# Attention's list scheduler: what a task waits for when its forerunner runs on the same engine

## The chip, the core and the metric

The program runs on one core of a Trainium2 chip, as one launch. The metric is the device time of the whole program in microseconds (us). The core has a matrix engine (TensorE, PE in the profile, its weight loads PEld), three element-wise engines (VectorE, DVE; ScalarE, ACT; GpSimd, POOL) and queues that issue DMAs, here above all SyncE's (SP). Each engine works through its own list of instructions in order; semaphores tie the lists together.

## The reference

Three layers follow each other; the output of one is the input of the next.

```python
scores = scale * np.matmul(q, k.transpose(0, 1, 3, 2))      # B, H, S, D = 4, 8, 576, 64
scores = np.where(causal, -1e9, scores) - rowmax
a = np.exp(scores); a /= a.sum(-1, keepdims=True) + 1e-09
local = np.matmul(a, v)
mem_out = (phi(q) @ M_prev) / (phi(q) @ z_prev + 1e-06)
attn = g * mem_out + (1 - g) * local
# x: 2304 tokens of 512 values
# layer 2: tokens with x @ w_skip > 0 go to the best of 8 experts (512 -> 1024 -> 512), weighted, added to x
# layer 3: leaky_relu(x @ w_in) @ w_out, 512 -> 2048 -> 512
```

## The kernel before

**Attention.** The 32 pairs of batch and head are worked on as 8 groups of 4 heads. For each group K and Q are loaded, split into a coarse part and a remainder (L592, L599), transposed on PE (L644, L647) and copied out of PSUM by ACT (L665, L666, L672). Each head then has two slots, one for the first two blocks of 128 rows and one for the other three. A slot runs this chain: PE makes scores (`mm`, L728); DVE adds the mask and takes row maxima (`mx`, L735) and writes them beside Q (`sp`, L747 and L752); PE transposes that (`q2t`, L759) and ACT copies it out (`q2e`, L764); PE makes the scores a second time, transposed and with the maximum taken off (L779, L781, the diagonal's mask L786 and L790); ACT takes the exponential (`exp`, L795); PE multiplies by V (`pv`, L817 and L820), with outputs 64 columns of the array wide, where nearly all other matmuls use 128. Two heads share a `pv` result. When it is complete, three DVE tasks follow each other: `f1` (L857, L859), `f2` (L864) and `f4` (L872, L874); POOL adds the two halves (L882).

Beside this, ACT, DVE and POOL turn the third layer's weights into another format (`conv_chunk`, L321 to L341); finished rows are routed to experts (`route_blk`, L925 to L946, with outputs 32 and 64 columns wide in L934 and L943; `route`, L972 to L1035). Towards the end the first expert's weights are split (L438, L444) and its first two tiles are computed (`early`, L485 to L531), with rows fetched by a gather (L1106, then transposed by L1119) that needs the table which the routing scatters write (L1035).

**What sets the order.** All of this is put down as 2159 tasks, each with an engine, an assumed duration, the tasks it depends on, a due time (`key`), and buffers that it takes and gives back. `Sched.order` plays them through: whenever an engine is free it starts the ready task with the smallest key for which buffers are free. A finished task makes its dependents ready `LAT` later: 550 ns after PE, 180 after ACT, 170 after DVE, 240 after POOL, 2300 after SP, or a latency of the task's own. The instructions are then issued in the order of these starts. The result is only an order for each engine; on the chip each instruction waits for its real semaphores.

The tasks that have a forerunner on their own engine are: on PE the `pv` steps of a slot and the first expert's products; on ACT the second copy of a K tile after the first (L666 after L665) and the successive `exp` of a slot; on DVE the `mx` of a slot, then `sp`, and `f1`, `f2`, `f4`; on POOL the routing scatters.

**After attention** come the experts (L1119 to L1266, in blocks chosen by the count of each expert's tokens) and the third layer (L1511 to L1617); their order doesn't go through the scheduler.

Of the kernel before, what the change touches and what calls it, by code (L numbers as in the profile page):

```python
# [34 lines left out]
SP = [[[(0, 0, 0, 128), (1, 128, 0, 256)]], [[(2, 0, 0, 384)], [(3, 0, 0, 512)], [(4, 0, 0, 256)], [(4, 0, 256, 320)]]]  # L35
# [28 lines left out]
class Sched:  # L64
# [9 lines left out]
    def order(self):  # L74
        ts, free = self.tasks, dict(self.free)
        users = [[] for _ in ts]
        left = [len(t[3]) for t in ts]
        for i, t in enumerate(ts):
            for d in t[3]:
                users[d].append(i)  # L80
        ready = {e: [] for e in self.LAT}
        busy = {e: 0.0 for e in self.LAT}
        ev, out = [], []

        def wake(i):
            heapq.heappush(ready[ts[i][0]], (ts[i][4], i))
        for i in range(len(ts)):
            if not left[i]:
                wake(i)
        now = 0.0  # L90
        while len(out) < len(ts):
            moved = True
            while moved:
                moved = False
                for e, rd in ready.items():
                    if busy[e] > now or not rd:
                        continue
                    skip = []
                    while rd:
                        key, i = heapq.heappop(rd)  # L100
                        eng, dur, fn, deps, _, take, give, lat = ts[i]
                        if all(free[p] >= 1 + (p == "s" and key > now + AHEAD) for p in take):
                            for p in take:
                                free[p] -= 1
                            end = now + dur
                            busy[e] = end
                            heapq.heappush(ev, (end, -1, None))
                            heapq.heappush(ev, (end + (self.LAT[e] if lat is None else lat), i, give))
                            out.append((now, i))
                            moved = True  # L110
                            break
                        skip.append((key, i))
                    for x in skip:
                        heapq.heappush(rd, x)
            if not ev:
                raise RuntimeError("stuck")
            now = ev[0][0]
            while ev and ev[0][0] <= now:
                _, i, give = heapq.heappop(ev)
                if i < 0:  # L120
                    continue
                for p in give:
                    free[p] += 1
                for u in users[i]:
                    left[u] -= 1
                    if not left[u]:
                        wake(u)
        self.end = now
        return [i for _, i in out]

# [1570 lines left out]
```

## Time and profile before

| | us |
|---|---|
| time, median of 3 runs | 864.18 (863.03 to 865.46) |
| the profiled execution's own time | 864.59 |
| its span, first to last instruction | 863.0 |
| PE busy | 829.5 (96%) |
| DVE, ACT, POOL busy | 612.4, 482.4, 193.4 |

The profile comes from one execution. Busy time counts instructions at work; a matmul's end is modelled, so that a row's end may lie beyond the next row's start, and the distance from start to start is the safer reading. In rows of a timeline a line's equal neighbours are merged (x12 is twelve of them), and the time in brackets is how long the engine sat idle ahead of them. A float32 matmul of `pv` is two records in the trace and one in the program. Attention lasts from 0 to about 298 us, mixed with the first expert's tiles to 329 us; the experts follow to 466 us, the third layer from there to the end.

### The profile page before, as it was taken

The numbers are of one execution on the slowest core, as the hardware profiler recorded it, in microseconds if no ns is written. First come the engines' busy times: TensorE is split into PE (matmuls) and PEld (weight loads), VectorE is DVE, ScalarE is ACT, GpSimd is POOL, SyncE is SP. The second block draws the span as 40 slices with busy tenths as digits, with TensorE's granted clock in tenths as the row PEclk, the third lists the DMA queues.
The fourth block names the chain that finished last, engine by engine and source line by source line (L and its number), as shares of the span: only waits on it lengthen the run. The fifth ranks groups of instructions, "written<-read, shape, count | busy, mean of one in ns | idle before, by whom it ended". The sixth has DMA issues, their size and how long they took to land. (4 is left out here: it accounts for less than half of the span.)

```text
span 863.0 us, 19512 instructions
## 1 busy us (share of the span) xinstructions
PE 829.5 (96%) x7368; PEld 739.8 (86%) x7368; DVE 612.4 (71%) x1739; ACT 482.4 (56%) x937; POOL 193.4 (22%) x262
## 2 busy tenths in 40 slices
PE   6999999999999898999989999999999999999997
PEld 5788888887887776677568999999999999999997
DVE  6878888788869964775674699665656565656564
ACT  8898978887866643765564465333333333333332
POOL 6545536445524423130220000000000000000000
PEclk9999999999999999999999999999999999999999
DMA  6867665856375768795833201010101010101000
GB/s 145 218 158 224 163 201 139 220 191 130 124 251 182 267 232 269 269 353 207 282 144 134 74 1 51 1 51 1 51 1 49 2 49 2 50 2 49 1 26 25
DMA packets 103946, 107.61 MB, mean 125 GB/s; under 512 B 69661, under 2 KB 69789, under 8 KB 103828
## 3 DMA queue, kind: packets, MB, share of 16 engines
q1 hardware_dynamic: 101190, 100.90, 37.5%
q0 software_dynamic: 2640, 5.21, 1.8%
q8 instruction: 67, 1.10, 0.5%
q14 instruction: 49, 0.40, 0.1%
HBM read 81.57 MB, written 25.86 MB: 124 GB/s over the span
## 5 line engine op out<-in xcount | busy, mean ns | idle before, releaser
L1616 PE MATMUL g<-sw,ah 128*128 128x256 f32 x448 | 126.0, 281 | 0.0
L1615 PE MATMUL g<-sw,ah 128*128 128x256 f32 x448 | 125.7, 281 | 0.0
L1567 DVE SCALAR_TENSOR_TENSOR ua<-ua 128x512 f32<-128x512 f32 x72 | 49.7, 690 | 80.2 <-ACT ua L1516 80.2
L1516 ACT ACTIVATE ah<-ua 128x384 fp32r<-128x384 f32 (+1 forms) x72 | 38.8, 539 | 110.4 <-PE g L1617 71.2
L1516 ACT ACTIVATE ua<-t 128x512 f32<-128x512 f32 x72 | 43.0, 597 | 101.0 <-PE t L1560 101.0
L735 DVE CUSTOM_DVE_ANT_0 v<-t,v 128x512 f32<-128x512 f32 (+4 forms) x160 | 75.5, 472 | 28.4 <-PE t L728 22.8
L1617 PE MATMUL g<-sw,al 128*128 128x256 f32 x320 | 89.8, 281 | 0.0
L1615 PEld LDWEIGHTS g<-sw,ah 128*128 128x128 f32 x448 | 84.4, 188 | 0.0
L1616 PEld LDWEIGHTS g<-sw,ah 128*128 128x128 f32 x448 | 84.3, 188 | 0.0
L795 ACT ACTIVATE pT<-t 128x384 f32<-128x384 f32 (+2 forms) x128 | 62.5, 503 | 23.8 <-PE t L786 12.8
L1557 PE MATMUL t<-x,v 128*128 128x256 f32 x288 | 71.9, 283 | 0.7 <-ACT x L1436 0.7
L1558 PE MATMUL t<-x,a 128*128 128x256 f32 x288 | 71.0, 280 | 0.5 <-DVE a L1103 0.5
L1558 PE MATMUL t<-x,v 128*128 128x256 f32 x288 | 71.1, 279 | 0.0
L1557 PE MATMUL t<-x,a 128*128 128x256 f32 x288 | 71.0, 280 | 0.0
L820 PE MATMUL pv<-vn,pT 128*64 128x65 f32 x1280 | 61.7, 231 | 0.6 <-issue 0.6
L1617 PEld LDWEIGHTS g<-sw,al 128*128 128x128 f32 x320 | 60.9, 190 | 0.0
L820 PEld LDWEIGHTS pv<-vn,pT 128*64 128x64 f32 x1280 | 47.0, 138 | 16.1 <-issue 11.1
L338 POOL TENSOR_TENSOR cg<-cg,v 128x512 int32<-128x512 int32 x32 | 42.5, 1329 | 65.3 <-issue 38.8
L1557 PEld LDWEIGHTS t<-x,v 128*128 128x128 f32 x288 | 54.3, 188 | 1.2 <-ACT x L1436 0.9
L1558 PEld LDWEIGHTS t<-x,a 128*128 128x128 f32 x288 | 54.1, 188 | 0.7 <-DVE a L1103 0.7
L1558 PEld LDWEIGHTS t<-x,v 128*128 128x128 f32 x288 | 54.1, 188 | 0.3
L1557 PEld LDWEIGHTS t<-x,a 128*128 128x128 f32 x288 | 54.1, 188 | 0.0
(371 smaller groups left out, 2313.2 us busy)
## 6 DMA issues: line engine op xcount, KB each, us to landing
c<-in_moe_w_dram SPq DMA_DIRECT2D x32, 512.0 KB
va<-in_moe_w_dram SPq DMA_DIRECT2D x21, 512.0 KB
v<-in_moe_w_in_dram SPq DMA_DIRECT2D x16, 512.0 KB
v<-in_moe_w_out_dram SPq DMA_DIRECT2D x16, 512.0 KB
xe<-x SPq DMA_DIRECT2D x18, 256.0 KB
out_dram<-xe SPq DMA_DIRECT2D x18, 256.0 KB
a<-in_k_dram SPq DMA_DIRECT2D x32, 128.0 KB
a<-in_q_dram SPq DMA_DIRECT2D x32, 128.0 KB
```

What stands on the lines that cost most here:

```text
L338: nc.gpsimd.tensor_tensor(u["g"], u["g"], u["s"], op=ALU.add)
L735: nc.vector.tensor_tensor_reduce(out=self.y[:R, 0:w], in0=s[:R, o:o + w], in1=self.mb[:R, max(0, MB[i] + c0):max(0, MB[i] + c0) + w], scal ...
L795: nc.scalar.activation(u["pT"][:, o1:o1 + w], u.pop(("t", p))[:, 0:w], AF.Exp, scale=0.125)
L820: nc.tensor.matmul(t[m:m + 64, o:o + 65], u["pT"][:, c + m:c + m + 64], vn[:, j, h], start=(j == 0), stop=(j == i))
L1516: tt_, cp = V.tensor_tensor, lambda o, i: A.activation(o, i, AF.Copy)
L1557: nc.tensor.matmul(o, wih[k][:, fs], xh[:, k], start=(k == 0), stop=False)
L1558: nc.tensor.matmul(o, wil[k][:, fs], xh[:, k], start=False, stop=False)
L1567: V.scalar_tensor_tensor(u, u, 0.01, u, op0=ALU.mult, op1=ALU.max)
L1615: nc.tensor.matmul(o, ah, wh, start=(p == z == 0), stop=False, skip_group_check=True)
L1616: nc.tensor.matmul(o, ah, wl, start=False, stop=False, skip_group_check=True)
L1617: nc.tensor.matmul(o, al, wh, start=False, stop=(p == 7), skip_group_check=True)
```

## The change

When a task ends, an event is now put down for its own engine at the very end of the task, beside the one after the latency. Dependents on the same engine (all but SP) are released by the first event, all others by the second, which also gives the buffers back.

```diff
-                            heapq.heappush(ev, (end, -1, None))
+                            heapq.heappush(ev, (end, -1 - i, ()))
                             heapq.heappush(ev, (end + (self.LAT[e] if lat is None else lat), i, give))
...
                 _, i, give = heapq.heappop(ev)
-                if i < 0:
-                    continue
+
+                own, i = i < 0, max(i, -1 - i)
                 for p in give:
                     free[p] += 1
                 for u in users[i]:
-                    left[u] -= 1
-                    if not left[u]:
-                        wake(u)
+                    if (ts[u][0] == ts[i][0] != "SP") == own:
+                        left[u] -= 1
+                        if not left[u]:
+                            wake(u)
```

No instruction is added or left out; the order on each engine changes. From the diff on, lines of the changed kernel have numbers higher by one (L820 is L821 there).

On PE, here is the third batch's last group, between the transposes of K and Q (L644) and those of the finished rows (L925). In the rows, pv is the result of the product with V, t any other PSUM tile, 64x65 its 64 columns of the array and 65 columns of V. Before:

```order
L644 MATMUL t<-idr,v_84 128x128 x4
L728 MATMUL t<-b_86 128x384
L820 MATMUL pv<-vn_90,pT 64x65 x6
L728 MATMUL t<-b_86 128x512
L820 MATMUL pv<-vn_90,pT 64x65 x8
L759 MATMUL t<-idr,v_84 66x128 x3
L728 MATMUL t<-b_86 128x256
L728 MATMUL t<-b_86 128x320
L820 MATMUL pv<-vn_90,pT 64x65 x2
L728 MATMUL t<-c_88 128x384
L817 MATMUL pv<-vn_90,pT 64x65 x5
L779 MATMUL t<-b_86 128x192
```

and in the changed kernel:

```order
L645 MATMUL t<-idr,v_84 128x128 x4
L760 MATMUL t<-idr,v_84 66x128 x3
L729 MATMUL t<-b_86 128x384
L818 MATMUL pv<-vn_90,pT 64x65 x5
L729 MATMUL t<-b_86 128x512
L821 MATMUL pv<-vn_90,pT 64x65 x12
L729 MATMUL t<-b_86 128x256
L729 MATMUL t<-b_86 128x320
L780 MATMUL t<-b_86 128x192
L782 MATMUL t<-q_4402,b_86 128x192
```

Four stretches of pv with other work between them have become two, one of them of twelve matmuls; L759 has moved ahead of the scores.

On DVE, near the end of attention, stand f1 (its last line is L859), f2 (L864) and f4 (L872, L874) of a pair of heads, with the row maxima (L735, an operation and a read of its accumulator) of other slots. Before:

```order
L857 TENSOR_TENSOR pv<-pv,ev 64x130
L859 SCALAR_TENSOR_TENSOR nl_99<-t,gl 128x3x2
L859 SCALAR_TENSOR_TENSOR nl_99<-pv,gl 128x3x2
L735 ISA v_85,m_98<-t,v_85 128x128
L735 ISA m_98 128x1
L735 ISA v_85,m_98<-t,v_85 128x256
L735 ISA m_98 128x1
L864 RECIPROCAL rl<-nl_99 128x12
L735 ISA v_85,m_97<-t,v_85 128x128
```

and in the changed kernel:

```order
L858 TENSOR_TENSOR pv<-pv,ev 64x130
L860 SCALAR_TENSOR_TENSOR nl_99<-t,gl 128x3x2
L860 SCALAR_TENSOR_TENSOR nl_99<-pv,gl 128x3x2
L865 RECIPROCAL rl<-nl_99 128x12
L873 TENSOR_TENSOR xb<-pv,rl 128x3x128
L875 TENSOR_TENSOR m_4865<-t,rl 128x384
L736 ISA v_85,m_98<-t,v_85 128x128
```

The three tasks of a pair of heads now follow each other with nothing between, and the next slot's maxima stand behind them.

## Rows read from the trace of the kernel before

**Rows 1.** The page: busy us and share of PE; granted clock in 40 slices.
```profile
PE 829.5 (96%) x7368; PEld 739.8 (86%) x7368; DVE 612.4 (71%) x1739; ACT 482.4 (56%) x937; POOL 193.4 (22%) x262
...
PEclk9999999999999999999999999999999999999999
```

**Rows 2.** Windows: length, busy of PE, PEld, DVE, ACT, POOL, clock, DMA share.
```profile
20.00:100.00 80.00, 78.20 (x904) 65.80 (x904) 64.49 (x246) 73.54 (x168) 43.47 (x54) 1.00 0.71 190
100.00:200.00 100.00, 97.19 (x1219) 82.72 (x1219) 84.29 (x331) 84.09 (x189) 51.93 (x64) 1.00 0.68 187
200.00:290.00 90.00, 86.97 (x1095) 74.19 (x1095) 73.62 (x282) 65.25 (x144) 43.43 (x48) 1.00 0.54 167
290.00:330.00 40.00, 35.74 (x263) 27.50 (x261) 28.84 (x89) 16.16 (x28) 11.65 (x16) 0.96 0.71 251
330.00:466.00 136.00, 126.86 (x584) 91.03 (x584) 89.02 (x104) 81.77 (x117) 29.70 (x21) 0.99 0.70 247
466.00:863.00 397.00, 391.60 (x3232) 387.03 (x3232) 258.75 (x651) 144.21 (x257) 0.97 (x1) 1.00 0.09 31
```

**Rows 3.** Waits of PE from 20 to 298 us: total us, times, longest.
```profile
PE t L1119 <- DMA xe<-xs,ixe: 2.2, 1, 2.2
...
PE t L759 <- DVE v L752: 0.6, 2, 0.3
```

**Rows 4.** Timeline of PE, 242 to 253 us: start, length, instruction.
```profile
242.65 0.29 PE L786 MATMUL t<-negi,tri 128*128 128x256 bf16 x1
242.70 0.74 PE L728 MATMUL t<-b 128*128 128x512 f32 x3
...
247.52 0.69 PE L820 MATMUL pv<-vn,pT 128*64 128x65 f32 x16
248.14 0.38 PE L759 MATMUL t<-idr,v 128*66 128x128 f32 x3
...
250.44 0.30 PE L781 MATMUL t<-q,b 66*128 66x320 f32 x1
250.58 0.28 PE L786 MATMUL t<-negi,tri 128*128 128x256 bf16 x1
250.80 0.57 PE L820 MATMUL pv<-vn,pT 128*64 128x65 f32 x12
251.30 0.41 PE L779 MATMUL t<-b 128*128 128x320 f32 x1
...
252.12 0.31 PE L781 MATMUL t<-q,b 66*128 66x320 f32 x1
252.36 0.45 PE L820 MATMUL pv<-vn,pT 128*64 128x65 f32 x8
252.75 0.38 PE L759 MATMUL t<-idr,v 128*66 128x128 f32 x3
```

**Rows 5.** Timeline of DVE, 274 to 288 us.
```profile
274.09 0.17 DVE L859 SCALAR_TENSOR_TENSOR nl<-pv,gl 128x6 f32<-128x6 f32 x1
274.17 0.28 DVE L735 CUSTOM_DVE_ANT_0 v<-t,v 128x128 f32<-128x128 f32 x1
274.38 0.08 DVE L735 DVE_READ_ACCUMULATOR2_ANT m<- 128x1 f32 x1
274.50 0.42 DVE L735 CUSTOM_DVE_ANT_0 v<-t,v 128x256 f32<-128x256 f32 x1
...
286.85 0.16 DVE L859 SCALAR_TENSOR_TENSOR nl<-pv,gl 128x6 f32<-128x6 f32 x1
287.04 0.23 DVE L864 RECIPROCAL rl<-nl 128x12 f32<-128x12 f32 x1
```

**Rows 6.** Waits of DVE from 20 to 290 us.
```profile
DVE v L735 <- PE t L728: 24.0, 31, 2.5
```

**Rows 7.** Timelines of POOL and DVE near the end of attention.
```profile
280.00 1.72 POOL L1035 DMA_INDIRECT tbl<-r_tok,r_sli  x1 [0.16 <-issue]
...
289.62 3.42 DVE L444 TENSOR_TENSOR v<-a,v 128x1024 fp32r<-128x1024 f32 x1 [0.24 <-ACT v L438]
```

## The prediction

> **What bounds the kernel now.** I read the page first, then windows, then the waits of PE, then its timeline from start to start. The page shows PE busy for 96% of the span and at the full clock nearly throughout [rows 1]; it is the engine to watch. The windows show that this holds in every stage: from 20 to 290 us, which is attention, PE is busy for 78.20 + 97.19 + 86.97 = 262.4 of 270 us, among the experts for 126.86 of 136 us, in the third layer for 391.60 of 397 us [rows 2]. So two things decide the change: how much PE work attention holds, and the 7.6 us in which PE is idle there. The last two stages are not reordered, and as PE fills them, what attention saves or loses should reach the end about one for one.
>
> Of the 7.6 us of idle time the longest piece is one wait of 2.2 us for a gather near the end; waits that name DVE's `sp` as the releaser are two, 0.6 us in all [rows 3]. A kernel with so few waits can't win much by losing them. What the order can still change is PE's own work, and that shows only in the timeline read from start to start. Three stretches of `pv` matmuls, of 16, 12 and 8, last 0.62, 0.50 and 0.39 us until the next kind of matmul starts [rows 4]. From 8 to 16 that is (0.62 - 0.39) / 8 = 0.029 us each; so 0.39 - 8 x 0.029 = 0.16 us comes once per stretch (0.15 by the stretch of 12). Going in costs too: L786 is followed by an L728 after 0.05 us but by `pv` after 0.22 us, and L781 by L786 after 0.14 us but by `pv` after 0.24 us [rows 4]. That is 0.10 to 0.17 us more. So each separate stretch of `pv` costs 0.25 to 0.33 us of PE beside its matmuls. The idle columns of the waits don't show it, since the modelled ends of the matmuls cover it.
>
> **The change part by part.** *Fewer stretches.* A `pv` step depends on the one before it. Before, 550 ns of assumed latency kept it back and the scheduler filled in other work; now it can follow at once. In the two orders of PE, up to the first branch, I count 128 stretches of `pv` before and 95 after, about 3 fewer in each 75 tasks all through attention. The routing's narrow stretches (L934, L943) rise from 27 to 33, some of them next to `pv`; stretches of 128-wide work between narrow ones fall from 144 to 113. So 31 go-and-return pairs go. I take 0.25 us, the lower value, because entries from other lines are not in these rows: 31 x 0.25 = -7.7 us, with ends at 31 x 0.21 = -6.5 (if an entry hides a further 0.04) and 31 x 0.33 = -10.2.
>
> The Trainium skill bears on the count, in "TensorEngine Tiling (Array Packing)", section "Tiling Modes", under "Key Properties": a change of the tiling mode, and not only of the tile, drains the engine. The 0.15 us at each stretch's end agrees. By the rule a change between 64 and 32 columns, or between 64 and 128 rows, counts as well; all changes of mode in the orders fall from 305 to 250, which is 27.5 pairs and would make the term -6.9 us.
>
> *DVE.* `f1`, `f2`, `f4` stand together in 64 of 64 places, before in 21. When the follower needs the result, it starts 0.19 us after its forerunner (286.85 to 287.04); an independent one starts after 0.08 us (274.09 to 274.17) [rows 5]. So 43 more dependent starts x 0.11 = 4.7 us of DVE. DVE is busy for 222.4 of these 270 us [rows 2] and stands 24.0 us waiting for PE's scores [rows 6]; that hides it, and I cost it at nothing. Without that cover it would be up to +4.7 us. In the same way L666 now stands right behind L665 and `exp` behind `exp` on ACT; the same operations in another order, no cost by itself.
>
> *ACT as the next limit.* From 20 to 100 us ACT is busy for 73.54 of 80 us [rows 2]. PE's saving there would be 7.7 x 80 / 270 = 2.3 us; with 6.5 us of ACT idle time it fits, but in-order queues at over 90% seldom close all gaps. I give back 1.0 us (ends 0 and 2.3).
>
> *Less room ahead of q2t.* The row maxima of a slot are a chain on DVE. After the accumulator read at 274.38 the next maximum starts at 274.50, 0.12 us later [rows 5]. The old latency of 170 ns stood in for that; now the scheduler counts nothing, and puts `q2t` (L759) earlier on PE than DVE can serve it. What is queued behind a waiting L759 is all of PE. Ends: -1 us (the other loops gain room, since `q2e` to the second scores lies further apart now) and 64 q2t x 0.2 = +12.8 us. I take +2.0 us, a quarter more than today's 7.6 us idle, since DVE has time to run ahead.
>
> *The gather at the end.* The last routing scatter of batch 2 is issued at 280.00 [rows 7], behind two adds and a `conv_chunk` operation; in the new order it follows the scatter before it directly, and the gather that PE waits for 2.2 us [rows 3] can come some 2.8 us earlier. But the remainder that the first expert's product needs stands behind the same weight splits on DVE (L444, 3.42 us at 289.62) [rows 7], at the same place in both orders, so PE would mostly wait for that instead. I take -0.5 us; ends 0 and -3.6 us (the 2.2 us, and 4% of 35.7 us of PE at the reduced clock of 290 to 330 us [rows 2]).
>
> *SP and POOL.* Dependents on SP keep their latency; loads shift by a few places. The second load of raw weights now stands behind one more store of converted weights; what it loads is not the first expert's but the next one's, so I cost the delay at nothing; if that room were gone, the store's own few us would show as a wait of the next expert.
>
> Sum: -7.7 + 1.0 + 2.0 - 0.5 = -5.2 us, against the profiled execution's 864.59 us (span 863.0 and 1.6 around it; 0.4 above the median of 864.18): 859.4 us.
>
> **Rivals.** *The saving becomes waiting (about 864.3 us).* PE gets to the same followers sooner, and ACT or DVE were what it would have met anyway. For it: ACT's 92% from 20 to 100 us, and `pv` itself now stands closer behind its `exp`. Against it: from 100 to 290 us ACT is busy for only 149 of 190 us, and DVE waits for PE, not PE for DVE [rows 2, 6]. Price: another 5 us of waits. An expert stage that waits for weights (DMA share 0.70 [rows 2]) would swallow the gain with the same result.
>
> *Slower: DVE's unplanned gaps (about 868 us).* A second-half slot has four links on its chain (three between maxima, one to `sp`), 4 x 0.12 = 0.48 us late, a first-half slot one, 0.12 us. If PE has no room at any q2t, 32 x 0.48 + 32 x 0.12 = 19.2 us; with six in ten, 11.5 us, and 11.5 - 7.7 + 1.0 - 0.5 = +4.3 us: 868.9 us; with half, 867. It beats the saving once waits at L760 pass 7.7 / 64 = 0.12 us each on average. For it: this chain is where the new rule takes away the assumed time, and the row shows a gap that is real. Against it: today L759 waits for DVE for 0.6 us in all, so most of them have room [rows 3].
>
> *More than forecast (about 855 us).* The gather's wait goes whole and ACT keeps pace: -7.7 + 0.8 - 2.6 = -9.5 us. It needs DVE's splits at the end to come earlier too, for which no row speaks.
>
> That the change does nothing is excluded as far as the order goes: the stretches do merge. Only that a stretch's fixed cost is a hidden wait, and not work, could undo it; then the first rival's time stands.
>
> **How the numbers follow.** Forecast 0.54, more than forecast 0.07, waits instead 0.21, slower 0.18. This kernel's runs differ by about 0.3% (2.6 us) without a change, so faster means under 861.6 us: 0.61; within: 0.21; slower, over 866.8 us: 0.18. The forecast's own range, from the terms' ends taken some at a time, is 854 to 863 us; the range for 8 in 10 adds the first rival and the lower half of the slower one, and the better case in part: 852 to 867.5 us.
>
> **What would show it.** In the changed profile: attention's PE busy time from 20 us on lower by 6 to 9 us, and stretches of `pv` at 0.029 us a matmul plus the same 0.15 us; L1119, the gathered rows' transposes, 3 to 7 us earlier; the third layer unchanged in length at 397 us. Waits of PE in attention of 8 to 11 us would confirm the third term; over 15 us, with L760 released by L753, would show the slower rival. ACT above 95% busy from 20 to 100 us with PE waiting for it would show the first. The prediction is wrong in its main step if the stretches fall by a quarter and PE's busy time doesn't.

## The result and the profile after

The changed kernel takes 877.74 us (873.11 to 879.91, 4 runs) against 864.82 us of the kernel before in the same comparison: ratio 1.0129, interval 1.0097 to 1.0161. By the two medians it is slower by 12.9 us (their quotient, 1.0149, lies within that interval). The forecast was 859.4 with a range of 852 to 867.5; the measured time is outside it. The profiled execution took 875.83 us with a span of 874.2.

The page of the changed kernel, to be laid beside [rows 1]: PE's busy time is nearly the same, but the granted clock now falls in three slices, the second, ninth and fifteenth of 21.9 us each.

```profile
PE 830.5 (95%) x7368; PEld 742.1 (85%) x7368; DVE 621.7 (71%) x1739; ACT 482.9 (55%) x937; POOL 197.6 (23%) x262
...
PEclk9899999989999989999999999999999999999999
```

Its windows, to be laid beside [rows 2] (the same columns). From 20 to 290 us PE is busy for 73.26 + 95.32 + 85.63 = 254.2 us where it was 262.4, so its idle time rises from 7.6 to 15.8 us; and the clock is 0.96, 0.95 and 0.98 in stages where it was 1.00.

```profile
20.00:100.00 80.00, 73.26 (x858) 62.44 (x858) 62.18 (x227) 70.34 (x157) 42.13 (x51) 0.96 0.65 177
100.00:200.00 100.00, 95.32 (x1163) 81.59 (x1161) 79.99 (x311) 80.44 (x185) 53.16 (x64) 0.95 0.67 184
200.00:290.00 90.00, 85.63 (x1045) 72.55 (x1041) 77.12 (x292) 64.43 (x145) 40.02 (x46) 0.98 0.51 170
290.00:330.00 40.00, 36.12 (x362) 28.97 (x363) 35.87 (x103) 21.42 (x38) 14.57 (x15) 0.91 0.68 238
```

Its waits of PE from 20 to 305 us, to be laid beside [rows 3]: what grew is the one line that the prediction bounded and took small. L760 (q2t, L759 before) waits for DVE's `sp` 9 times instead of 2, 7.0 us instead of 0.6.

```profile
PE t L760 <- DVE v L753: 7.0, 9, 1.1
PE pv L821 <- ACT pT L796: 1.1, 1, 1.1
PE t L760 <- DVE nl L860: 0.9, 1, 0.9
```

How such a wait arises is seen on DVE, in the timeline from 207 to 212 us. The last raw scores of a slot (L729) start on PE at 207.64. DVE takes the maxima at 209.32 and 210.83, and between these two, without a break, the five instructions of another pair of heads' f1, f2 and f4 (L860 to L875). This is what the new rule allows: a follower is ready at once, so that it can start ahead of whatever else is ready with a later due time. `sp` (L753) ends at 211.77; PE had come to L760 at 211.09 and stood for 0.74 us.

```profile
209.32 0.41 DVE L736 CUSTOM_DVE_ANT_0 v<-t,v 64x256 f32<-64x256 f32 x1
...
209.67 0.15 DVE L860 SCALAR_TENSOR_TENSOR nl<-t,gl 128x4 f32<-128x4 f32 x1
209.75 0.14 DVE L860 SCALAR_TENSOR_TENSOR nl<-pv,gl 128x4 f32<-128x4 f32 x1
209.92 0.20 DVE L865 RECIPROCAL rl<-nl 128x8 f32<-128x8 f32 x1
210.16 0.42 DVE L873 TENSOR_TENSOR xb<-pv,rl 128x256 f32<-128x256 f32 x1
210.50 0.42 DVE L875 TENSOR_TENSOR m<-t,rl 128x256 f32<-128x256 f32 x1
210.83 0.53 DVE L736 CUSTOM_DVE_ANT_0 v<-t,v,m 64x320 f32<-64x320 f32 x1
```

In the kernel before the same slot had one task between the same two maxima as well, a longer one (1.59 us), yet its q2t stood for only 0.29 us: its last raw scores start at 197.22 and PE comes to L759 at 202.17, 4.95 us later, where it is now 211.09 - 207.64 = 3.45 us. Over the 32 slots of the second half of the rows, this distance from the last raw scores to q2t falls from a median of 4.07 us to 3.25, and its lowest tenth from 3.02 to 2.41; in the first half the lowest tenth falls from 2.61 to 2.01, though the median rises there from 3.49 to 4.23 (all taken from the two traces).

The waits have a second price. Behind some of them PE runs at half clock (1.2 of 2.4 GHz). PE's timeline of the changed kernel from 211 to 220 us: two waits of 0.74 and 1.02 us for L753, and from 218.62 on the matmuls take nearly twice as long. Twelve of `pv` go from 212.46 to 212.96 (0.50 us to the next start) at the full clock, and from 219.31 to 220.16 (0.85 us) at half.

```profile
211.83 0.37 PE L760 MATMUL t<-idr,v 128*66 128x128 f32 x3 [0.74 <-DVE v L753]
212.04 0.49 PE L648 MATMUL t<-idr,v 128*128 128x128 f32 x4
212.46 0.57 PE L821 MATMUL pv<-vn,pT 128*64 128x65 f32 x12
212.96 0.49 PE L729 MATMUL t<-c 128*128 128x128 f32 x2
...
217.00 0.32 PE L760 MATMUL t<-idr,v 128*66 128x128 f32 x2 [1.02 <-DVE v L753]
...
219.31 0.92 PE L821 MATMUL pv<-vn,pT 128*64 128x65 f32 x12
220.16 0.58 PE L780 MATMUL t<-c 128*128 128x256 f32 x1
```

There are four such stretches up to 311 us: 6.83 us from 30.89, 10.24 from 170.83, 3.41 from 218.62 and 6.83 from 303.95, the last one beginning inside a wait of 2.88 us that ends at 305.06. Before there was one, 3.41 us from 292.82, beginning in the last 0.21 us of the wait for the gathered rows. Windows around the longest show what stands on either side: ahead of it the full clock with PE idle for 1.8 of 20.8 us, of which the last two waits are 0.51 and 0.79 us, then half clock with PE busy throughout.

```profile
150.00:170.80 20.80, 19.02 (x237) 16.28 (x236) 18.55 (x65) 16.85 (x37) 14.19 (x17) 1.00 0.70 189
170.80:181.10 10.30, 10.30 (x74) 8.68 (x74) 3.77 (x17) 7.20 (x17) 3.43 (x4) 0.50 0.66 199
```

So the account goes by three sums, from the start to the first product of the experts' main loop (L1206, now L1207). One window of each kernel, before and after:

```profile
0.00:330.64 330.64, 310.99 (x3552) 261.79 (x3553) 265.23 (x990) 256.69 (x564) 162.70 (x240) 0.99 0.65 188
```

```profile
0.00:343.39 343.39, 313.44 (x3553) 265.42 (x3553) 274.35 (x990) 257.16 (x564) 165.93 (x241) 0.96 0.62 180
```

Idle time goes from 330.64 - 310.99 = 19.65 to 29.95 us: +10.3. Time at half clock goes from 3.4 to 27.3 us; at 0.45 us lost for each (measured below, in the run with stalls) that is +10.7. What is left is PE's work at full clock: 310.99 - 0.45 x 3.4 = 309.5 before, 313.44 - 0.45 x 27.3 = 301.2 after: -8.3. Together +12.7 us. Behind this point the expert stage is 1.5 us shorter, since a fall of the clock that the kernel before has at 381.57 us (3.41 us) is gone, and the third layer has the same length to 0.01 us (399.75 from the first L1434, now L1435, to the end). That makes the 11.2 us between the two spans.

### The profile page after: what moved, and what is told of

Its sections match the earlier page's. It is cut to its first block, busy times and chain, and to the rows that moved or that the text cites. A ratio compares the mean times of both kernels' runs of the same rounds, so it can differ in the third digit from the quotient of the medians.

```text
span 874.2 us, 19517 instructions
## 1 busy us (share of the span) xinstructions
PE 830.5 (95%) x7368; PEld 742.1 (85%) x7368; DVE 621.7 (71%) x1739; ACT 482.9 (55%) x937; POOL 197.6 (23%) x262
## 5 line engine op out<-in xcount | busy, mean ns | idle before, releaser
L736 DVE CUSTOM_DVE_ANT_0 v<-t,v 128x512 f32<-128x512 f32 (+4 forms) x160 | 75.5, 472 | 27.7 <-PE t L729 20.8
L796 ACT ACTIVATE pT<-t 128x384 f32<-128x384 f32 (+2 forms) x128 | 58.7, 504 | 33.6 <-PE t L787 29.5
L821 PE MATMUL pv<-vn,pT 128*64 128x65 f32 x1280 | 56.4, 233 | 4.9 <-DVE xb L873 3.6
L821 PEld LDWEIGHTS pv<-vn,pT 128*64 128x64 f32 x1280 | 45.8, 142 | 17.6 <-issue 11.2
```

Source lines behind the costliest of these rows:

```text
L736: nc.vector.tensor_tensor_reduce(out=self.y[:R, 0:w], in0=s[:R, o:o + w], in1=self.mb[:R, max(0, MB[i] + c0):max(0, MB[i] + c0) + w], scal ...
L796: nc.scalar.activation(u["pT"][:, o1:o1 + w], u.pop(("t", p))[:, 0:w], AF.Exp, scale=0.125)
L821: nc.tensor.matmul(t[m:m + 64, o:o + 65], u["pT"][:, c + m:c + m + 64], vn[:, j, h], start=(j == 0), stop=(j == i))
```

## The experiments

All times are medians, the ratio is to the kernel before in the same job (its medians there: 864.23 for the rules for DVE, for PE and for all but DVE and for the 560 alone; 865.53 for the rule for ACT, the 540, the 560 with 200 and the three additions; 865.13 for the 420, the 300, the six additions and the filled waits; 864.64 for the last two). "Idle" and "half clock" are of the profiled execution, up to L1206 or what answers to it, as in the account above; that is one execution of several, and where it lies far from the median this is said.

**The rule for one engine, or all but one.** The line that decides is narrowed, first to DVE:

```diff
-                    if (ts[u][0] == ts[i][0] != "SP") == own:
+                    if (ts[u][0] == ts[i][0] and ts[i][0] in ('DVE',)) == own:
```

> The new rule for DVE tasks alone; PE, ACT and POOL keep the old latency. Theory D (the rows of maxima lose their assumed 170 ns a link, PE reaches q2t too early, and its stops pull the clock down): 872 to 880 us, waits of L760 for L753 of 5 us or more, 15 us or more at half clock. Theory P (the PE rule does the harm, by putting pv ahead of urgent work): 862 to 867 us. Theory N (the constants were fitted to one order, and any other order of like distance costs as much): 870 to 880 us, with waits spread over many lines.

Measured: 878.37 us, ratio 1.0179 (1.0147 to 1.0210). DVE's rule alone makes the whole loss. PE keeps 124 stretches of `pv`, and its work at full clock doesn't fall (312.4 us, 2.9 more than before). The half clock, 17.1 us, adds 6.1 us, and idle time 5.3. L760 waits longer than with the whole change; some other waits got shorter, as the idle time grew by less:

```profile
PE t L760 <- DVE v L753: 10.0, 11, 2.3
```

```diff
+                    if (ts[u][0] == ts[i][0] and ts[i][0] in ('PE',)) == own:
```

> The new rule for PE tasks alone; 99 stretches of pv instead of 128. Theory D: the saving of the stretches without the waits, 857 to 862 us, waits of L760 for L753 under 2 us. Theory P: 872 us or more. Theory N: 870 to 880 us.

Measured: 866.58 us, ratio 1.0013 (0.9985 to 1.0040), with 99 stretches. No loss, but no gain either: PE's work at full clock falls to 301.5 us (-8.0), and the half clock, 23.9 us, with 3.0 us more of idle time, takes it back.

```diff
+                    if (ts[u][0] == ts[i][0] and ts[i][0] in ('PE', 'ACT', 'POOL')) == own:
```

> The new rule for PE, ACT and POOL, the old one for DVE; 88 stretches of pv. Theory D: 856 to 861 us, the fastest of the four. Theory P: 872 us or more. Theory N: 870 to 880 us.

Measured: 867.34 us, ratio 1.0011 (0.9976 to 1.0047). Leaving DVE out of the change gives back 10 us. The work is the least of all (299.0 us at 88 stretches), idle 27.5 and half clock 23.9 us are nearly as high as in the changed kernel. Its ten executions tell the clock's part apart: three took 859.5 to 859.7 us at a mean granted clock of 0.994 to 0.998, the other seven 866.0 to 870.5 at 0.981 to 0.988 (the profiled one 869.76). Where the clock stays up, some 4.7 us are won on the kernel before; mostly it does not.

```diff
+                    if (ts[u][0] == ts[i][0] and ts[i][0] in ('ACT',)) == own:
```

> The own-engine rule for ACT's tasks alone, the part that no run had by itself: 123 pv stretches, the 5% and 10% points of the room ahead of q2t 1.89 and 1.89 us. Theory C: about the time of the kernel before, 860 to 868, as the room is nearly that of before and few stretches go. If ACT's rule is a second cause beside DVE's: 870 or more.

Measured: 865.81 us, ratio 1.0000 (0.9973 to 1.0028): no second cause.

**Does any other order lose?** The old rule, with PE's 550 as 560 (in the second run as 540, in the third as 560 with DVE's 170 as 200):

```diff
-    LAT = {"PE": 550.0, "ACT": 180.0, "DVE": 170.0, "POOL": 240.0, "SP": 2300.0}
+    LAT = {"PE": 560.0, "ACT": 180.0, "DVE": 170.0, "POOL": 240.0, "SP": 2300.0}
```

> The old rule; only the assumed latency after PE is 560 ns instead of 550, which moves PE's tasks by 1.4 places on average (the change moves them by 2.8) and leaves 131 stretches of pv. Theories D and P: 862 to 868 us. Theory N: 869 us or more, since this order too is not the one that the constants were fitted to.

Measured: 858.88 us, ratio 0.9934 (0.9918 to 0.9951), faster than both kernels. The work is not less (311.9 us, 131 stretches), but idle time falls from 19.6 to 12.6 us and the clock doesn't fall before 375 us:

```profile
0.00:324.47 324.47, 311.87 (x3553) 262.69 (x3553) 261.21 (x990) 255.60 (x564) 166.45 (x241) 1.00 0.66 191
```

```diff
+    LAT = {"PE": 540.0, "ACT": 180.0, "DVE": 170.0, "POOL": 240.0, "SP": 2300.0}
```

> The kernel before with TensorE's 550 ns changed to 540 and the old rule: a second small reshuffle (129 pv stretches, the 5% and 10% points of the room ahead of q2t 1.68 and 1.98 us, before 1.89 and 2.01). Theory C (TensorE's waits, and the clock behind them, make the loss; orders with the same room cost about the same): 857 to 868. Theory N (the first control at 560 was luck, and orders off the tuned one scatter by 10 us): 870 or more, or anything outside 857 to 868.

Measured: 862.87 us, ratio 0.9963 (0.9939 to 0.9986).

```diff
+    LAT = {"PE": 560.0, "ACT": 180.0, "DVE": 200.0, "POOL": 240.0, "SP": 2300.0}
```

> The old rule with two more careful numbers: 560 ns behind TensorE instead of 550 and 200 behind DVE instead of 170 (127 pv stretches, room ahead of q2t 1.89 and 1.99 us at 5% and 10%, room of pv behind its scores 2.52 and 3.80 us where before has 1.96 and 3.74). Theory C: as few waits as the control at 560, under 13 us of TensorE's standing still up to the second layer, hardly any half clock, 855 to 862. If the control's 858.9 was luck of one order: 862 to 870.

Measured: 864.56 us, ratio 0.9993 (0.9964 to 1.0023), idle 16.4 us: a miss. More careful numbers don't add up to fewer waits; 560 alone is a good order and not the start of a direction. But none of the three reshuffles loses, so the 13 us are not what any change of order costs.

**Room given back.** The changed kernel with 420 ns instead of 170 from DVE to the other engines:

```diff
+    LAT = {"PE": 550.0, "ACT": 180.0, "DVE": 420.0, "POOL": 240.0, "SP": 2300.0}
```

> The changed kernel with one number changed: other engines follow a DVE task after 420 ns in the plan instead of 170, DVE's own tasks still after 0. In the task order the 10% point of TensorE's planned work between a slot's raw scores and its q2t goes from 1.62 back to 2.14 us (before: 2.01), and the pv stretches stay at 96 (before 128, changed 95). Theory C (the waits of TensorE for DVE's chain, and the clock that falls to half after them, are the loss): L760 waits for L753 fall from 7.0 to under 2.5 us, the time at half clock from 27 to under 10 us, and the run takes 855 to 862, below before, as the stretches' saving of about 6 us is then left. Theory P (the own-engine rule on TensorE is itself harmful): 870 or more, with or without those waits. Theory N (any other order than the tuned one costs some 10 us): 870 or more.

Measured: 866.61 us, ratio 1.0010 (0.9988 to 1.0032). The 96 stretches stay and 11 us come back; the L760 waits are 2.9 us instead of 7.0. The forecast's other half fails: in the profiled execution the clock is still at half for 27.3 us, behind what is left of these waits and behind others (the next largest are below). That execution was the slowest of the ten (871.69 us at a mean clock of 0.981; the others 0.983 to 0.994), but the median too is at the time before and not below it.

```profile
PE t L760 <- DVE v L753: 2.9, 5, 1.1
PE t L729 <- DVE m L875: 2.1, 2, 1.3
PE t L645 <- ACT pT L796: 1.9, 3, 0.8
PE t L729 <- issue: 1.2, 2, 0.7
```

And the rule for PE alone, with 300 from DVE:

```diff
+    LAT = {"PE": 550.0, "ACT": 180.0, "DVE": 300.0, "POOL": 240.0, "SP": 2300.0}
```

> The own-engine rule for TensorE alone (102 pv stretches), with 300 ns instead of 170 from DVE to everybody, DVE's own tasks included: the 10% point of the room ahead of q2t is 2.21 us, the largest of these kernels. The rule for TensorE alone took 866.6 with 27.3 us at half clock and 2.9 us of L760 waits for L753. Theory C: those waits go under 1.5 us, the time at half clock under 10 us, and the run takes 853 to 859. If the falls of the clock have nothing to do with the waits for DVE, the clock is at half for 20 us or more as it was, and the run takes 863 to 868.

Measured: 866.47 us, ratio 1.0030 (0.9998 to 1.0062): a miss. The half clock goes down to 10.2 us, about as expected, but the waits only move: L760 behind L753 is still 2.3 us in two waits, and idle time stays at 22.3. Here the clock is not all: the four executions at 0.998 to 1.000 took 864.4 to 866.9 us, about the time of the kernel before.

**What a wait costs beside its own length.** The kernel before, with work that nobody reads put on DVE ahead of `sp` in four slots; in the second run three additions in place of six:

```diff
+            if (n, hf, h) in ((2, 1, 1), (4, 1, 1), (5, 1, 1), (6, 1, 1)):
+                for _ in range(6):
+                    nc.vector.tensor_tensor(out=self.y, in0=self.mb, in1=self.mb, op=ALU.add)
```

> The kernel before with nothing moved, but six 128x512 additions more on DVE (some 3.3 us) ahead of the sum of maxima in four of the 64 slots, whose results nobody reads, so that TensorE's next q2t is late by 1 to 3 us at four places (near 100, 165, 205 and 245 us), each at full clock before. Theory C: after most of these waits the clock is at half for 3.4 to 10.2 us, where the kernel before has none up to 290 us, and the time rises by the waits (4 to 10 us) and by half of that time besides: 873 to 885. If waits cost no more than themselves: no half clock there, and 866 to 874.

Measured: 895.03 us, ratio 1.0345 (1.0304 to 1.0387), more than any theory gave: +29.9 us. The waits for `sp` are 12.3 us up to 298 us (waits row below), the largest 2.44, 2.83, 4.52 and 2.14; at each of these four the clock falls, for 10.24, 10.24, 10.24 and 13.65 us, in the second and third case before the wait is over. The windows show the first: a wait that ends at 99.11, then half clock with PE busy all the time.

```profile
PE t L762 <- DVE v L755: 12.3, 5, 4.5
```

```profile
95.00:100.00 5.00, 2.56 (x35) 2.32 (x32) 4.79 (x13) 2.52 (x7) 0.62 (x1) 1.00 0.59 132
100.00:105.00 5.00, 5.00 (x34) 4.54 (x34) 3.96 (x19) 3.72 (x10) 3.74 (x5) 0.52 0.79 199
105.00:110.00 5.00, 5.00 (x41) 4.21 (x37) 2.34 (x8) 2.62 (x7) 0.33 (x1) 0.50 0.48 112
...
0.00:361.36 361.36, 330.91 (x3552) 278.94 (x3553) 278.27 (x1014) 258.69 (x564) 163.64 (x240) 0.93 0.59 172
```

PE does the same work as before, so the last row prices the clock: busy 330.91 - 310.99 = 19.9 us more, for 47.8 - 3.4 = 44.4 us more at half clock, 0.45 us for each (0.48 if the 3.0 us more are left out in which PE still stood idle at half clock). The twelve `pv` above agree: (0.85 - 0.50) / 0.85 = 0.41.

```diff
-                for _ in range(6):
+                for _ in range(3):
```

> The stalls of the run with six additions halved: three additions (six took 4.31 us, so 2.15 us) in the same four slots of the kernel before, so that TensorE waits there for 0.3 to 2.4 us, the length of the waits in the changed kernel. Theory C: the clock falls to half at two or more of the four places, for 3.4 to 10.2 us each, and the run takes 869 to 882, more than the 2 to 6 us of the waits. If only waits of 2.4 us and more, as those of six additions, bring the clock down: no fall there or one, and 866 to 870.

Measured: 872.40 us, ratio 1.0081 (1.0048 to 1.0114). Half a miss. The additions made PE wait at three of the four places, for at most 0.90, 0.66 and 2.32 us; at the fourth, near 241 us, PE had enough other work and didn't wait. Only the 2.32 brought the clock down at its place (10.24 us from 207.24). A wait of 0.87 us at 292.96, where nothing was added, did not either, and the other fall (6.83 us from 299.40) stands between two waits for the gathered rows. So a single wait of under 1 us needn't bring the clock down. In the changed kernel the short ones ahead of its first three falls come two and more at a time. But one of just over 1 us can stand alone: in the two runs on DVE's chains below, one of 1.18 us that ends at 210.77 comes before 6.83 us at half clock (from 211.33), and one of 1.12 us that ends at 211.36 goes with 10.24 us (from 211.02). Why one wait brings the clock down and another of nearly the same length does not stays open.

**The waits filled.** The changed kernel in its own order, with idle work for PE ahead of twelve q2t:

```diff
+            if (n, hf, h) in ((0, 0, 3), (1, 0, 1), (1, 0, 2), (1, 1, 3), (2, 0, 0), (3, 1, 1), (3, 0, 2), (4, 1, 1), (5, 1, 1), (5, 0, 3), (7, 0, 1), (7, 0, 3)):
+                for _ in range(10):
+                    nc.tensor.transpose(t[:66, 384:512], self.idr[:, :66], self.idr)
```

> The changed kernel with the same order, and ten transposes more of a constant (0.06 us each, into a part of the tile that nobody reads) ahead of the q2t of twelve slots, the ones at which TensorE waited for 0.3 to 1.15 us: TensorE works through the wait instead of standing still, and nothing gets ready earlier. Theory C: two of the four falls of the clock (10.2 us at 170 and 3.4 at 218, both right behind such waits) go or get shorter, and the run takes 868 to 873 against 877.7. If the waits cost only their own length and the clock falls for other reasons: 877 to 882, the fillers that outlast their wait added.

Measured: 874.95 us, ratio 1.0119 (1.0090 to 1.0148), 2.8 us less than the changed kernel although PE does 120 matmuls more. Both falls behind such waits, at 170.83 and 218.62, are gone. The first of the four is shorter (3.41 us from 26.74); the one at 303.95 is gone too, and one of 6.83 us at 282.74 is new. One pair of windows shows the place of the longest (filled kernel first, then the changed one):

```profile
168.00:182.00 14.00, 13.04 (x160) 11.31 (x160) 10.02 (x42) 10.96 (x27) 5.09 (x6) 1.00 0.74 195
```

```profile
168.00:182.00 14.00, 12.74 (x102) 10.81 (x102) 6.97 (x29) 9.48 (x22) 4.80 (x6) 0.63 0.63 178
```

Up to the experts the half clock goes from 27.3 to 10.2 us (-7.7 at 0.45) and the idle time from 29.9 to 24.9 (-5.0); the filling costs 11.7 us of work, 0.10 us a piece where 0.06 was assumed, which is why so little is left of it.

**Which of DVE's chains.** DVE's rule in two parts, first the chain ahead of q2t, then everything else:

```diff
+                    if (ts[u][0] == ts[i][0] == "DVE" and ts[u][2].__name__ in ("mx", "sp")) == own:
```

> The own-engine rule only between a slot's row maxima and from the last of them to sp on DVE (the four-link chain ahead of q2t), 170 ns everywhere else on DVE and the old rule on the other engines: 124 pv stretches. Theory D1 (the chain ahead of q2t is what DVE's rule spoils: its links take longer than the plan now says): near DVE's rule alone, 873 to 879, with 6 us or more of L760 waits for L753. Theory D2 (it is the other chains, the three gate steps that now run without a break ahead of the maxima, and the routing's): 861 to 868, L760 waits for L753 under 3 us.

Measured: 869.11 us, ratio 1.0047 (1.0033 to 1.0062).

```diff
+                    if (ts[u][0] == ts[i][0] == "DVE" and ts[u][2].__name__ not in ("mx", "sp")) == own:
```

> The complement on DVE: the own-engine rule for all of DVE's chains but the one ahead of q2t (gate steps, routing's scatter chains), old rule elsewhere: 126 pv stretches. Theory D1: 861 to 868, L760 waits for L753 under 3 us. Theory D2: 873 to 879, with 6 us or more of them.

Measured: 871.96 us, ratio 1.0083 (1.0058 to 1.0107). Neither theory holds alone: the chain ahead of q2t costs 4.5 us, the gate steps (`f1`, `f2`, `f4`) and the routing together 7.3, in sum 11.8 of the 14.1 us that all of DVE's rule cost. L760's waits for L753 are 4.3 and 3.2 us (first row of each, chain first; the second profile is of the slowest of six executions, 878.76 us):

```profile
PE t L760 <- DVE v L753: 4.3, 7, 1.2
```

```profile
PE t L760 <- DVE v L753: 3.2, 5, 1.6
PE t L1026 <- DVE oh L1019: 1.1, 1, 1.1
```

## Why the prediction was wrong

- **Fewer stretches: right.** Forecast -7.7 us; PE's work falls by 8.3. Over the 13 orders with unchanged work (before, after and eleven runs), work at full clock against the number of `pv` stretches lies on a line of 0.31 us a stretch (correlation 0.96, 88 stretches at 299.0 us to 131 at 311.9); the rows had given 0.25 to 0.33. Row by row it stands in the changed kernel as before: twelve of `pv` take 0.50 us to the next start (212.46 to 212.96, above) as they did [rows 4]. The Trainium skill ("TensorEngine Tiling (Array Packing)", section "Tiling Modes", "Key Properties") says that a change of the mode drains the engine. By a count of all changes of mode the term was -6.9 us; the 8.3 measured doesn't tell that count from the count of stretches.
- **"Less room ahead of q2t": here it failed.** The step said +2.0 us, "since DVE has time to run ahead", out of ends that went to +12.8. PE's idle time rose by 10.3 us up to the experts, L760's waits for L753 by 6.4 of it up to 305 us. That DVE has idle time on the whole (24.0 us waiting for PE [rows 6], still 19.8 us in the changed kernel) does not give it room in this chain: at the places that count PE now comes to q2t sooner after the last raw scores (2.41 us against 3.02 in the lowest tenth of the second half of the rows).
- **The clock: not in the sum.** The prediction charged a wait with its own length. 23.9 us more at half clock cost 10.7 us, as much as the idle time itself. Without it the account would have come out at +2 us. In the trace of the kernel before, the one fall in attention, at 292.82 us with a wait of 2.2 us [rows 2, 3], had shown that the two can go together; the prediction priced it for the gather alone.
- **DVE "at nothing": wrong in its reason.** The 43 more dependent starts were weighed as DVE time. Nowhere did the term ask where they stand: f1, f2 and f4 now come in one piece ahead of a maximum. The run with the rule for them and for the routing's chains, and not for the chain ahead of q2t, lost 7.3 us; how that divides between gate steps and routing was not tried.
- **ACT as the next limit (+1.0), the gather (-0.5):** from 20 to 100 us, where the ACT term was placed, PE's waits that name ACT go from 0.7 to 1.6 us, which is its size; from 20 to 298 us they fall from 4.2 to 3.4. The gather's wait went, but L1120 came at 301.09 instead of 293.03, 8.1 us later and not 3 to 7 earlier; L821 waited 2.88 us at 305.06 instead.
- **The slower rival** named the right place (L760, released by L753), and its sign to look for came true: idle over 15 us from 20 to 290. Its break-even was 0.12 us for each of 64 q2t, 7.7 us; measured are 7.0. By waits alone it would have been a draw; it was the clock behind them that made 877.7 out of its 868. And its chain is less than half of the cause (4.5 of the 11.8 us).

What stays open: why fewer stretches go along with more idle time also without DVE's rule (27.5 us at 88 stretches, 22.7 at 99, 22.3 at 102, against 12.6 to 19.6 in the orders with 127 to 131). No run with under 105 stretches kept its idle time below 22 us. That longer pieces of `pv` hold back the scores that ACT and DVE live on would fit, but was not tried.

## What to carry to other kernels

Where one engine is busy for 97% of a stage, price a wait of that engine twice: its own length, and the clock behind it. Here 10.3 us of waits brought 10.7 us of clock, and a saving of 8.3 us of real work was lost against them. A scheduler's latency is not only a forecast of when data is there; it is also the spacing that keeps long side chains from closing up ahead of a short urgent one, so take it away engine by engine and time each. And a control with a trifling change (550 to 560) belongs to every study of an order: it was the fastest kernel of all.

## What the runs showed of the hardware

In the changed kernel the clock fell behind short waits of PE: groups of 0.4 to 1.1 us (four ahead of 30.89 us, two each ahead of 170.83 and 218.62), and inside one of 2.88 us that ends at 305.06. Before, one wait of 2.2 us went with the only fall in that stage [rows 2, 3]. In all sixteen traces each fall up to 400 us has a wait of PE of at least 0.5 us close ahead of it or around its start; but waits of 0.66 to 0.90 us also passed without a fall, in the run with three additions. The clock stayed at half for 3.41, 6.83, 10.24 or 13.65 us, even where PE was busy without a gap in the stretch (10.30 of 10.30 us from 170.80). The Trainium skill ("TensorE: Matmul & The Clock Gate", Part 1, "What's actually happening") says that the lower clock is the default and activity releases it; the trace agrees in that PE comes back to 2.4 GHz after such a stretch of work. What half clock costs, 0.45 us per us, is a little less than the half of it that the two levels would give; part of the difference is time at half clock in which PE stood idle anyway. The number of such stretches differs between executions of one kernel: the mean granted clock was 0.978 to 0.990 in the four of the changed kernel, 0.998 to 1.000 in the four of the control at 560, and 0.989 to 0.998 in 26 of the kernel before, whose spans lie between 861.1 and 868.1 us.
